# Laying out octets by batch with TensorE from a kept tile, in place of copies between partitions by DMA

## The chip, the cores and the metric

The kernel runs on one core of one Trainium2 chip. The metric is the device time of the execution in microseconds (us), taken as the median of the runs. The engines are named as in the profile: PE is TensorE (PEld its weight loads), DVE is VectorE, ACT is ScalarE, POOL is GpSimd and SP is SyncE, which here only issues DMAs.

## The reference

The input is q, k and v of shape (8 batches, 8 heads, 576 tokens, 64). An attention with exponential features gives x of shape (8, 576, 512), and a spectral mix then works on x:

```
X = rfft(x, axis=1)                                  # along the tokens
Y[:, :64] = Xr*w_r - Xi*w_i + 1j*(Xr*w_i + Xi*w_r)   # 64 modes, a 512 x 512 matrix each
y = irfft(Y, n=576, axis=1)
u = x + y
out = u + relu(u @ w_ch)
```

The weights w_r and w_i are 64 matrices of 512 x 512 each, 64 MB each in float32. All that follows concerns the second half, from the mix to the output.

## The kernel before, in words

**The two halves.** The first 300 us or so work through sixteen units of attention; each ends in a few matmuls that give the low frequencies of its tokens (tile XT). In between, and after the last unit, run the mixes.

**Mixes and octets.** A mix (function `mix`) multiplies one group g of 128 input channels by one load of weights of 1 MB (eight modes, real or imaginary). Two mixes (i = 0, 1) for each of four groups g make up the 512 output channels of an octet o: eight modes, with real and imaginary part and eight batches, so 128 rows in the order (mode and part, batch). There are eight octets. Of the 64 mixes twenty come after the last unit: the twelve for g = 3 of octets 0 to 5, then eight for octets 6 and 7. In the order of these twenty, counted from 0, octet o < 6 ends with mix 2 o + 1, octet 6 with mix 15 and octet 7 with mix 19. The loop `while mixq` goes through them; `left` is the number of mixes still to come.

**Weights.** `next_w` issues the load of the next weights from POOL's queue into a ring of nine tiles (`pw`, tag "wt") of 8 KB a partition. A load waits until a tile of the ring is free, which is when the mix that read it is done. The tiles `zall`, `yall` and `yl` come from the same ring; each takes its slot when it is first written.

**What an octet's end does.** The sum of the octet is put together in `yst` (two DVE adds of 256 columns). It is turned by four PE transposes into `yT` (one copy by ACT, one by DVE) and multiplied by w_ch (`wchb`, eight matmuls) to give z, which ACT and DVE cast into `zst`. The rows of `yst` and `zst` are in the order (mode and part, batch), but the inverse transform needs the modes on the partitions and one batch at a time. `put` does this by DMA: 128 rows of 1 KB go to sixteen partitions of `yall` (or `zall`), eight rows in each, one for each batch. For octets 6 and 7 further copies go into `yl`.

**Chunks and fills.** The tokens are 36 chunks, four pairs of batches bp by nine n. Before the sums can be put in, each chunk is turned and multiplied by w_ch (`hold`, a step of four transposes and four matmuls; its result goes to `xw`). After octet 5, every chunk takes up octets 0 to 5 (`Absorb`): one matmul from the inverse table CI or CD by `yall` of its batch, added to x by DVE (`keep_x`), and one by `zall`, added to `xw` by PE and ACT, or, for fourteen chunks that are left aside, by ACT and POOL (`keep_w`). The eight chunks of bp 0 with n < 8 are `early` and take octet 6 as well (112 rows instead of 96). Three chunks (`only_x`, `only_w`) keep the product with w_ch in PSUM until the sums come. All these steps stand in one list, `todo`, and `fill(n)` does n of them after a mix; n is worked out from what is left, so that the list is empty before the last mix. After the last mix, `Last` adds octets 6 and 7 and stores.

**Order.** Each engine does its instructions in the order of the program. PSUM has four single banks ("pt") and two double ones ("pp") in this part.

Of the kernel before, what the change touches and what calls it, by code (L numbers as in the profile page):

```python
# [11 lines left out]
BF16 = mybir.dt.bfloat16  # L12
# [5 lines left out]
B_, H_, S_, D_ = 8, 8, 576, 64  # L18
# [25 lines left out]
def kernel(  # L44
# [14 lines left out]
    pe, dve, act = (InOrder(tc, e) for e in (nc.tensor, nc.vector, nc.scalar))  # L59
    pool, sp = InOrder(tc, nc.gpsimd), InOrder(tc, nc.sync)  # L60
# [23 lines left out]
    pw = pw_cm.__enter__()  # L84
# [255 lines left out]
    def wload(g, w):  # L340
        wt = home(g, w)
        o, i = w // 2, w % 2
        w = (moe_w_r, moe_w_i)[i]
        pool.dma_start(
            wt.rearrange("p m r e -> p m (r e)"),
            w[MG * o:MG * o + MG, g * 128:(g + 1) * 128, :].rearrange(
                "m (p r) e -> p m (r e)", r=2))
        return wt
# [10 lines left out]
    def next_w(n):  # L359
        for _ in range(n):  # L360
            if wq:
                key = wq.pop(0)
                wts[key] = wload(*key)
# [25 lines left out]
    wchb = const.tile([128, 4, 512], BF16, name="wchb")  # L389
    CF = const.tile([128, 6, 2, 2, 32], BF16, name="CF")  # L390
    side = const.tile([128, 2, 4], F32, name="side")
    ident_b = const.tile([128, 128], BF16, name="ident_b")
# [32 lines left out]
    for t in range(3):  # L425
        r = slice(32 * t, 32 * t + 32)
        dve.tensor_scalar_mul(out=minus[r], in0=ident_f[r, r], scalar1=-1.0)
    every = mf[0:96, 0:32]
    for t in range(3):
        r = slice(32 * t, 32 * t + 32)  # L430
# [30 lines left out]
    def mix(g, w, wt, XT, bank):  # L461

        o, i = w // 2, w % 2
        late = g >= 2 and o >= 6
        first, last = i == 0 and not (late and g == 3), i == 1 and not (late and g == 2)
        if first:
            pys[o] = bank()
        py = pys[o]
        for r in range(2):
            for j in range(4):  # L470
                pe.matmul(
                    py[32 * j:32 * j + 32, :],
                    lhsT=XT[:, i, r, :, :, :, 4 * o + j].rearrange("p t x b -> p (t x b)"),
                    rhs=wt[:, j, r, :], start=(first and r == 0), stop=(last and r == 1),
                )
        if last and g == 0:
            act.copy(yacc[:, o, :], pys.pop(o))
        elif last and g < NG - 1:
            dve.tensor_tensor(
                out=yacc[:, o, :], in0=pys.pop(o), in1=yacc[:, o, :], op=ALU.add)  # L480
# [19 lines left out]
    def unit(i):  # L500
        return units[i] if 0 <= i < len(units) else None

    for n in range(-2, len(units) + 1):
        P, Q, K, R = (unit(n + i) for i in (-1, 0, 1, 2))
# [77 lines left out]
    def bank(shape=(128, DMODEL), dt=F32):  # L582
        return pst.tile(list(shape), dt, name="pt", tag="pt")
# [4 lines left out]
    pb_cm = tc.tile_pool(name="pb", bufs=2)  # L588
    pb = pb_cm.__enter__()
    xw = pb.tile([128, NP, 9, DMODEL], BF16, name="xw", bufs=1)  # L590
    zall = pw.tile([128, B_, DMODEL], BF16, name="zall", tag="wt")
    yall = pw.tile([128, B_, DMODEL], BF16, name="yall", tag="wt")
    yl = pw.tile([128, B_, DMODEL], BF16, name="yl", tag="wt")
# [85 lines left out]
    class Channels:  # L679
# [29 lines left out]
        def hold(self, pf):  # L709
            for g in range(NG):  # L710
                pe.matmul(pf, lhsT=self.xT[:, g, :], rhs=wchb[:, g, :],
                          start=(g == 0), stop=False)
# [68 lines left out]
    ch = [Channels(*c) for c in chunks]  # L781
    ab = [Absorb(*c) for c in chunks]
    K = len(ch) - 3
    full = sorted(ab[:K], key=lambda c: c.early)
    spare = []
    for c in full[0:28:2]:
        c.aside = True
# [17 lines left out]
        ch[i].hold(ab[i].q)  # L805

    todo = [ch[0].turn] + [lambda i=i: hold(i) for i in range(len(ch))]
    todo += [c.only_x for c in ab[K:]] + [c.only_w for c in ab[K:]] + [c.all for c in full]
    A = 3 * 3 + K

    def fill(n):
        for _ in range(n):
            if todo:
                todo.pop(0)()

    def put(src, o, dst, copies):
        if o < 7:
            sp.dma_start(dst[16 * o:16 * o + 16], src)
        if o > 5:
            for s in copies:  # L820
                r = 32 * s + 16 * (o - 6)
                (pool if o == 6 else sp).dma_start(yl[r:r + 16], src)


    class Last:
# [97 lines left out]
    while mixq:  # L923
        key = mixq.pop(0)
        g, o, i = key[0], key[1] // 2, key[1] % 2
        if key not in wts:
            next_w(1)
        if not mixq:
            assert not todo
            for c in seq[:2]:  # L930
                c.base(1)
            for c in (seq[0], seq[2]):
                c.base(0)
        mix(*key, wts.pop(key), XTb[g % 2], bank)
        next_w(1)
        left = len(mixq)
        if left > 8:
            n = -(-max(len(todo) - A - 2, 0) // (left - 8))
        elif left == 8:
            n = 2  # L940
        else:
            n = math.ceil(len(todo) / max(left - 0.6, 0.4)) if left else 0
        if g == NG - 1 and i == 1:
            end = left == 0
            py = pys.pop(o)
            yst = pb.tile([128, DMODEL], BF16, name="yst")
            pt = [bank([128, 2, 128], BF16) for h in range(2)]
            yT = [pb.tile([128, 2, 128], BF16, name=f"yT{h}") for h in range(2)]
            for h in range(2):
                dve.tensor_tensor(out=yst[:, H * h:H * h + H], in0=py[:, H * h:H * h + H],  # L950
                                  in1=yacc[:, o, H * h:H * h + H], op=ALU.add)
            put(yst, o, yall, (0, 2))
            if o < 5:
                fill(min(n, 1))
            for h in range(2):
                for dc in range(2):
                    pe.transpose(pt[h][:, dc, :],
                                 yst[:, H * h + 128 * dc:H * h + 128 * dc + 128], ident_b)
                if h:
                    dve.tensor_copy(yT[h], pt[h])  # L960
                else:
                    act.copy(yT[h], pt[h])
            if o < 5:
                fill(min(n - 1, 1))
            elif end:
                seq[0].straight(0)
                seq[0].keep_p()
                seq[2].straight(0, (0,))
            cut = (slice(0, 384), slice(384, DMODEL))
            pz = [bank([128, e.stop - e.start]) for e in cut]  # L970
            for e in range(2):
                for h in range(2):
                    for dc in range(2):
                        pe.matmul(
                            pz[e], lhsT=yT[h][:, dc, :], rhs=wchb[:, 2 * h + dc, cut[e]],
                            start=(h == dc == 0), stop=(h == dc == 1))
            zst = pb.tile([128, DMODEL], BF16, name="zst")
            act.copy(zst[:, cut[0]], pz[0])
            dve.tensor_copy(zst[:, cut[1]], pz[1])
            put(zst, o, zall, (1, 3))  # L980
            fill(max(n - 2, 0) if o < 5 else n)
        else:
            fill(n)
    assert not todo
# [18 lines left out]
    for g in range(3, len(seq)):  # L1003
        s, ts = seq[g], [seq[i] for i in ahead[g - 3:g - 2]]
# [49 lines left out]
```

## Time and profile before

| | |
|---|---|
| median of 3 runs | 439.06 us (438.94 to 439.31) |
| the profiled execution | 440.25 us, of which 438.5 us are the profile's span |
| mean granted clock of TensorE | 0.906 |
| PE, DVE, ACT, POOL busy | 332.0, 296.4, 279.4, 113.0 us |
| DMA | 99.55 MB moved, 227 GB/s on average |
| mix 0, mix 12, mix 19 start at | 302.1, 368.5, 403.1 us |
| copies yall<-yst and zall<-zst | 7 of 128 KB each, first issued at 320.40, last at 386.80 us |

The profile is one execution. Its span runs from the first instruction to the last; start times in the text are microseconds from the start of the span. A row's duration holds the time in which a matmul drains, during which the next one already runs, so that TensorE's rate is read from start to start.

### The profile page before, as it was taken

The page shows a single profiled execution, that of the slowest core. Times are in us where ns is not written, and L with a number is a line of the kernel's source. Part 1 is how long each engine was busy: PE and PEld are TensorE (multiplying, and loading weights), DVE is VectorE, ACT ScalarE, POOL GpSimd, SP SyncE. Part 2 cuts the span into 40 slices and gives each one's busy share as a digit, 9 for nine tenths or more (in the row PEclk, how much of TensorE's full clock was granted, in tenths as well). Part 3 has the DMA queues.
Part 4 walks back from the last instruction along what each step waited for, and adds up shares of the span by engine and source line. Part 5 has one row for each costly group of instructions (what it writes and reads, how often), then busy time and mean ns, then how long its engine had stood idle before and what let it go on. Part 6 is the DMA issues. An engine that isn't in the chain of part 4 may idle for free.

```text
span 438.5 us, 10107 instructions
## 1 busy us (share of the span) xinstructions
PE 332.0 (76%) x4190; PEld 202.1 (46%) x4233; DVE 296.4 (68%) x583; ACT 279.4 (64%) x478; POOL 113.0 (26%) x151
## 2 busy tenths in 40 slices
PE   2687678688687687687787787284789999998993
PEld 1355456465465465455465555152444554333320
DVE  5667776765786877976986888243784333886684
ACT  3786786776986886875875876210553442665781
POOL 6232132113221222221222221121101111483072
PEclk9998796789998999996996998876899999999996
DMA  9999999999999999999999999999999999996787
GB/s 213 209 212 210 237 212 237 237 212 248 228 211 239 225 228 232 237 215 235 232 217 239 210 239 211 238 213 212 212 215 223 219 222 224 212 219 135 242 361 309
DMA packets 51710, 99.55 MB, mean 227 GB/s; under 512 B 2512, under 2 KB 13648, under 8 KB 51664
## 3 DMA queue, kind: packets, MB, share of 16 engines
q0 software_dynamic: 45232, 85.86, 99.7%
q1 hardware_dynamic: 6272, 12.98, 8.5%
q8 instruction: 33, 0.54, 0.5%
q14 instruction: 13, 0.11, 0.1%
q10 hardware_dynamic: 160, 0.07, 0.1%
HBM read 163.64 MB, written 9.44 MB: 395 GB/s over the span
## 4 chain that ended last, share of the span: by engine, by line
PE 43%; DVE 22%; ACT 18%; DMA 10%; issue 5%; POOL 0%; POOLq 0%; ACTq 0%; DVEq 0%
PE pt L37 17%; PE one L37 14%; DMA wt<-in_moe_w_r_dram 8%; PE two L37 8%; ACT AB L37 7%; DVE m L37 6%; DVE mk L37 6%; PE pp L37 4%; ACT AQ L37 3%; ACT XT L37 3%; DVE xs L37 2%; DVE XT L37 2%; DMA qb<-in_q_dram 2%; ACT qT L37 1%; DVE yacc L37 1%
## 5 line engine op out<-in xcount | busy, mean ns | idle before, releaser
L37 ACT ACTIVATE AB<-two 128x1024 bf16<-128x1024 f32 x64 | 62.0, 1024 | 10.6 <-DVE mk L37 7.2
L37 ACT ACTIVATE AQ<-two 128x1024 bf16<-128x1024 f32 x64 | 62.6, 1043 | 2.0 <-PE two L37 1.8
L37 ACT CAST xw<-pt 128x512 bf16<-128x512 f32 x50 | 29.4, 588 | 41.9 <-PE pt L37 41.8
L37 DVE TENSOR_REDUCE m<-two 128x8 f32<-128x1024 f32 x32 | 39.2, 1224 | 15.8 <-PE two L37 15.7
L37 DVE TENSOR_TENSOR va<-vn,ee 128x1152 bf16<-128x1152 f32 x32 | 42.0, 1355 | 8.2 <-DMA vn<-in_v_dram 8.2
L37 DVE TENSOR_REDUCE mk<-two 128x8 f32<-128x1024 f32 x32 | 38.9, 1218 | 7.7 <-PE two L37 7.7
L37 POOL DMA_DIRECT2D wt<-in_moe_w_i_dram x28 | 21.0, 750 | 86.4 <-PE pt L37 37.7
L37 POOL DMA_DIRECT2D wt<-in_moe_w_r_dram x30 | 22.5, 751 | 69.2 <-PE one L37 30.7
L37 PE MATMUL pt<-wchb,xT 128*128 128x512 bf16 x127 | 35.6, 393 | 5.2 <-DVE xT L37 3.5
L37 PEld LDWEIGHTS <-xs 128*128 128x128 bf16 x624 | 31.6, 103 | 12.6 <-issue 7.3
L37 PE MATMUL two<-w2blk,qT 128*128 128x256 bf16 x128 | 22.1, 301 | 20.2 <-ACT AB L37 8.4
L37 ACT COPY qT<-one 128x512 bf16<-128x512 bf16 (+1 forms) x32 | 19.3, 641 | 27.5 <-PE one L37 27.2
L37 PEld LDWEIGHTS <-qT 128*128 128x128 bf16 x144 | 14.6, 103 | 36.8 <-issue 33.2
L37 PE MATMUL one<-wt,XT 128*32 128x512 bf16 x304 | 27.5, 452 | 4.9 <-DMA wt<-in_moe_w_i_dram 3.3
L37 PE MATMUL two<-mT,minus 96*128 96x512 bf16 x64 | 28.5, 446 | 3.2 <-issue 1.5
L37 PEld LDWEIGHTS <-AQ 128*128 128x128 bf16 x512 | 25.8, 111 | 8.8 <-issue 5.6
L37 PE MATMUL one<-kvz,AQ 128*128 128x65 bf16 x512 | 28.4, 212 | 1.2 <-ACT qT L37 0.8
L37 DVE COPY xT<-pt 128x512 bf16<-128x512 bf16 x36 | 17.0, 472 | 17.8 <-PE pt L37 17.8
L37 PE MATMUL one<-va,AB 64*128 64x65 bf16 x1024 | 22.5, 199 | 8.3 <-DVE va L37 8.3
L37 DVE RECIPROCAL rd<-one 128x6 f32<-128x6 f32 x48 | 9.4, 196 | 27.6 <-PE one L37 27.5
L37 DVE TENSOR_TENSOR xs<-one,rd 128x384 bf16<-128x384 f32 x48 | 26.7, 557 | 1.6
L37 POOL DMA_DIRECT2D kb<-in_k_dram x16 | 11.4, 714 | 62.2 <-PE one L37 57.2
(151 smaller groups left out, 719.3 us busy)
## 6 DMA issues: line engine op xcount, KB each, us to landing
wt<-in_moe_w_r_dram POOLq DMA_DIRECT2D x30, 1024.0 KB, 28.1
wt<-in_moe_w_i_dram POOLq DMA_DIRECT2D x28, 1024.0 KB, 28.4
out_dram<-of SPq DMA_DIRECT2D x16, 512.0 KB, 4.0
vn<-in_v_dram POOLq DMA_DIRECT2D x14, 576.0 KB, 24.6
kb<-in_k_dram POOLq DMA_DIRECT2D x16, 288.0 KB, 20.4
qb<-in_q_dram POOLq DMA_DIRECT2D x16, 288.0 KB, 18.3
xs<-in_moe_w_i_dram POOLq DMA_DIRECT2D x2, 1024.0 KB, 23.1
vn<-in_v_dram SPq DMA_DIRECT2D x2, 576.0 KB, 4.6
```

The source lines that it names most:

```text
L37: ins = f(*args, **kwargs)
```

## The change

A new tile `yTa` of the weight ring keeps the turned y of octets 0 to 5, and of octet 6 for batches 0 and 1, in the order (channels, batch, octet, mode and part). At the end of octets 0 to 5 the two copies out of PSUM write there instead of into `yT`, with the rows taken apart by batch; there is no product with w_ch, no `zst`, and no DMA. For octet 6, which still makes z for `yl`, two small DVE copies add its part.

A new step `relay(b)` makes `yall` and `zall` of batch b, with 96 rows (112 for batches 0 and 1): four transposes of the kept columns back into rows, which DVE copies to `yall`, and four matmuls of the same columns by w_ch, which ACT casts to `zall`. The eight relays are put into the list: those of batches 7 and 6 ahead of the three chunks held in PSUM, each other one right before the first chunk that needs it.

The list of chunks is sorted so that all nine of bp 0 come last (before, chunk (0, 8) came earlier). The steps of a fill at the end of octets 0 to 4, which stood partly between the sum and the transposes and partly before the product, now all come after the copies. Three calls of `next_w` are left out (after mixes 0, 10 and 11), so that slots come free for `yTa`, `yall` and `zall`; the two last loads are issued one mix later for it.

```diff
+    yTa = pw.tile([128, 4, B_, 7, 16], BF16, name="yTa", tag="wt")
     zall = pw.tile([128, B_, DMODEL], BF16, name="zall", tag="wt")
...
-    full = sorted(ab[:K], key=lambda c: c.early)
+    full = sorted(ab[:K], key=lambda c: c.bp == 0)
+
+    def relay(b):
+
+        at = slice(0, 6 + (b < 2))
+        n = 16 * at.stop
+        cols = [yTa[:, dc, b, at].rearrange("p o k -> p (o k)") for dc in range(4)]
+        pt, pz = bank([128, 4, 128], BF16), bank()
+        for dc in range(4):
+            pe.transpose(pt[:n, dc, :], cols[dc], ident_b)
+        for dc in range(4):
+            pe.matmul(pz[:n], lhsT=cols[dc], rhs=wchb[:, dc, :],
+                      start=(dc == 0), stop=(dc == 3))
+        dve.tensor_copy(yall[:n, b], pt[:n].rearrange("p c e -> p (c e)"))
+        act.copy(zall[:n, b], pz[:n])
...
-    todo += [c.only_x for c in ab[K:]] + [c.only_w for c in ab[K:]] + [c.all for c in full]
-    A = 3 * 3 + K
+    order2 = [c.only_x for c in ab[K:]] + [c.only_w for c in ab[K:]]
+    laid = {7, 6}
+    tail = [lambda: relay(7), lambda: relay(6)] + order2
+    for c in full:
+        bs = {2 * c.bp, 2 * c.bp + 1} if c.n == 8 else {2 * c.bp + c.n // 4}
+        tail += [lambda b=b: relay(b) for b in sorted(bs - laid)] + [c.all]
+        laid |= bs
+    A = 3 + len(tail)
+    todo += tail
...
-    def put(src, o, dst, copies):
-        if o < 7:
-            sp.dma_start(dst[16 * o:16 * o + 16], src)
-        if o > 5:
-            for s in copies:
-                r = 32 * s + 16 * (o - 6)
-                (pool if o == 6 else sp).dma_start(yl[r:r + 16], src)
+    def put(src, o, copies):
+        for s in copies:
+            r = 32 * s + 16 * (o - 6)
+            (pool if o == 6 else sp).dma_start(yl[r:r + 16], src)
...
-        next_w(1)
         left = len(mixq)
+        if left not in (19, 9, 8):
+            next_w(1)
...
-            put(yst, o, yall, (0, 2))
-            if o < 5:
-                fill(min(n, 1))
+            if o > 5:
+                put(yst, o, (0, 2))
             for h in range(2):
                 for dc in range(2):
                     pe.transpose(pt[h][:, dc, :],
                                  yst[:, H * h + 128 * dc:H * h + 128 * dc + 128], ident_b)
+                src = pt[h].rearrange("p c (k b) -> p c b k", b=B_)
+                into = yTa[:, 2 * h:2 * h + 2, :, o] if o < 6 else None
                 if h:
-                    dve.tensor_copy(yT[h], pt[h])
+                    dve.tensor_copy(*((into, src) if o < 6 else (yT[h], pt[h])))
                 else:
-                    act.copy(yT[h], pt[h])
-            if o < 5:
-                fill(min(n - 1, 1))
-            elif end:
+                    act.copy(*((into, src) if o < 6 else (yT[h], pt[h])))
+            if o < 6:
+                fill(n)
+                continue
+            if o == 6:
+                for h in range(2):
+                    dve.tensor_copy(
+                        yTa[:, 2 * h:2 * h + 2, 0:2, 6],
+                        yT[h].rearrange("p c (k b) -> p c b k", b=B_)[:, :, 0:2])
+            if end:
...
-            put(zst, o, zall, (1, 3))
-            fill(max(n - 2, 0) if o < 5 else n)
+            put(zst, o, (1, 3))
+            fill(n)
```

More of the change, by code (lines that the diff above doesn't have):

```diff
@@ L947 @@
             pt = [bank([128, 2, 128], BF16) for h in range(2)]
-            yT = [pb.tile([128, 2, 128], BF16, name=f"yT{h}") for h in range(2)]
+            yT = [pb.tile([128, 2, 128], BF16, name=f"yT{h}") if o > 5 else None
+                  for h in range(2)]
             for h in range(2):
```

## The prediction

> **What bounds the kernel now.** I read the page's queue table first, then the chain that ended last in order of time, then busy time by stretches, then the single rows of TensorE, VectorE and ScalarE around the places that the change touches.
>
> The queue table makes the weight stream look like the bound:
>
> ```profile
> q0 software_dynamic: 45232, 85.86, 99.7%
> q1 hardware_dynamic: 6272, 12.98, 8.5%
> ```
>
> The queue that carries the weights (q0) is busy for the whole span. But what ends last is read from the chain, and there the DMA stops at 302 us; from then on TensorE carries it, in pieces like the second of these (start, length, both in us), with short ones of VectorE and ScalarE between:
>
> ```profile
> 265.36 36.71 DMA wt<-in_moe_w_r_dram
> ...
> 357.56 5.21 PE pt L37 x41
> ```
>
> I number the last twenty mixes 0 (starts 302.1) to 19 (starts 403.1). Stage A is mixes 0 to 12, in which octets 0 to 5 end (after mixes 1, 3, 5, 7, 9, 11); stage B is from mix 12 to mix 19, where the octets' sums are put into the chunks. By stretches (us, then PE, PEld, DVE, ACT, POOL busy, clock, DMA share, GB/s):
>
> ```profile
> 351.07:360.47 9.40, 9.12 (x77) 4.83 (x77) 3.63 (x10) 4.27 (x8) 1.48 (x2) 1.00 1.12 220
> ...
> 373.95:403.11 29.16, 27.40 (x160) 10.29 (x160) 22.83 (x38) 20.65 (x38) 18.29 (x18) 1.00 1.03 203
> ```
>
> TensorE is busy 9.12 of 9.40 us in stage A with VectorE and ScalarE under half, and 27.4 of 29.2 in stage B, with VectorE (22.8) and ScalarE (20.7) close behind. So every TensorE microsecond added or removed here counts. The weights are only just ahead: the last load is issued at 369.47 and lands 32.8 us later, at 402.3, under a microsecond before mix 19; but no mix after number 0 waits for one.
>
> **What is removed, stage A.** Each of octets 0 to 5 loses eight z matmuls, two zst casts and two copies by DMA. TensorE's rows in order of time at an octet's end, with a hold step put between mix and y transposes (octet 4, from 355.02) and with nothing between (octet 5, from 363.35):
>
> ```profile
> 355.02 0.67 PE L37 MATMUL pt<-wt,XT 128*32 128x512 bf16 x8
> 355.62 0.40 PE L37 MATMUL pt<-ident_b,xs 128*128 128x128 bf16 x4
> 355.86 0.81 PE L37 MATMUL pt<-wchb,xT 128*128 128x512 bf16 x3
> 356.72 0.39 PE L37 MATMUL pt<-ident_b,yst 128*128 128x128 bf16 x4
> 356.94 0.39 PE L37 MATMUL pt<-ident_b,xs 128*128 128x128 bf16 x4
> 357.56 1.02 PE L37 MATMUL pt<-wchb,xT 128*128 128x512 bf16 x4 [0.23 <-ACT xw L37]
> ...
> 363.35 0.66 PE L37 MATMUL pt<-wt,XT 128*32 128x512 bf16 x8
> 364.54 0.61 PE L37 MATMUL pt<-ident_b,yst 128*128 128x128 bf16 x4 [0.54 <-DVE yst L37]
> 365.35 1.05 PE L37 MATMUL pt<-wchb,yT 128*128 128x384 bf16 x8 [0.19 <-ACT yT L37]
> 366.23 0.39 PE L37 MATMUL pt<-ident_b,xs 128*128 128x128 bf16 x4
> 366.45 1.03 PE L37 MATMUL pt<-wchb,xT 128*128 128x512 bf16 x4
> 367.32 0.39 PE L37 MATMUL pt<-ident_b,xs 128*128 128x128 bf16 x4
> ```
>
> Counted from start to next start (a row's time holds the drain, which overlaps): eight z matmuls 0.88 (365.35 to 366.23), four transposes 0.22, four 512-column matmuls 0.87 (366.45 to 367.32), so 0.217 each; a hold step is 0.22 + 0.87 = 1.09; a mix with the gap ahead of it 0.69. Two mixes, six hold steps, four y transposes, the z matmuls and 0.39 of wait for a bank (from 356.94 + 0.22 to 357.56, ended by ACT) make 1.38 + 6.54 + 0.22 + 0.88 + 0.39 = 9.41; the stretch from mix 8 to mix 10 is 9.40. So the accounting closes.
>
> The diff also takes away the hold step between mix and y transposes: the fills of octets 0 to 4 now come after both copies. TensorE then waits for VectorE's sums, as octet 5 does already: the mix's eight matmuls are issued by 363.95 (0.60 after their start, as 355.02 to 355.62), the transposes end at 365.15, and the next matmul could start 0.17 before that, at 364.98 (as 356.94 lies 0.17 before the end of the row at 356.72): 1.04 for the octet's end instead of 0.22. The wait lets ScalarE empty its bank, so the 0.39 goes. New cycle 1.38 + 6.54 + 1.04 = 8.96, a gain of 0.44 for each of octets 2, 3 and 4: 1.3. Octet 5 had nothing between: it gains 0.88 + 0.19 = 1.07. Octets 0 and 1 lie in 302 to 332 where VectorE works on the inverse tables (22.6 of 30.2 busy) and is often what ends TensorE's wait; I take 0.3 each. Stage A: **-3.0 us** (from -1.1, octet 5 alone, to -5.5, all six by 0.88 and that wait).
>
> The copies from turned y to the kept tile, with a strided PSUM side, stay at 0.29 on DVE and 0.38 on ACT or grow a little (the strided xT copies take 0.64 where the plain ones take 0.42); both engines idle half of this stage. Nothing. The fourteen copies of 128 KB (1.8 MB, some 8 us of the stream's 220 GB/s) leave the 16 DMA engines: weights land earlier, which is worth nothing as no mix waits for them. SP has nothing else queued there before the yl copies and the stores. The three skipped loads give the slots for the kept tile and for yall and zall; the loads (3,10) to (2,15) move one mix earlier or stay, the last is released after mix 13 instead of 12, but by then the stream still has five loads before it: nothing. On POOL they stand ahead of the sums of the chunks that leave xw aside, as before.
>
> **What is added, stage B.** Eight relays, each four transposes (0.22), four 512-column matmuls (0.87), a DVE copy of turned y (0.41, as a plain xT copy) and an ACT cast of z (0.59, as an xw cast). TensorE alone: 8 x 1.09 = 8.7. More comes from where they stand: six stand right ahead of the chunk that reads their result. The state of the two other engines when such a relay begins, r, is read where TensorE is through with an odd chunk, at r = 383.27:
>
> ```profile
> 383.31 0.68 DVE L37 TENSOR_TENSOR xs<-pt,xs 128x512 bf16<-128x512 f32 x1
> ```
> ```profile
> 383.91 0.59 ACT L37 CAST xw<-pt 128x512 bf16<-128x512 f32 x1
> ```
>
> DVE is free at r + 0.72 and has yall at r + 1.13, just behind the last z matmul (r + 1.09): hidden. ACT is free at r + 1.23; the z product is ready at r + 1.25; cast 0.59, so zall is there at r + 1.9 and the chunk's z matmul, which without a relay would start at r + 0.22 (behind one y matmul, since these chunks leave xw aside), starts at r + 1.94. So an exposed relay costs 1.72. Four are fully exposed (batches 4, 5, 2, 3): 6.9; batch 1 stands before a chunk with one more matmul in between: 1.5; batch 0 is the last item of its fill and mix 17 covers the cast: 1.1; batches 7 and 6 stand together and cover each other, with a little wait for banks while the held sums occupy one of four: 2.4. Sum 11.9. Something comes back: chunks go by VectorE's 0.60 each (380.30, 380.90, 381.50 in its rows), TensorE needs 0.54 (five matmuls of 0.217 for two); 33 x 0.06 = 2.0 of such waiting is in stage B, and each relay lets VectorE catch up. I take back 1.2. The two small DVE copies for octet 6 lie beside its z matmuls: nothing, and 0.3 without that cover. Stage B: **+10.7 us** (from 8.7 - 2.0 = 6.7, all latency hidden, to 15.4, every relay at 1.72 and its transposes at the 0.10 of a weight load instead of 0.055).
>
> Against the row (four transposes in 0.22) stands a rule of the Trainium skill, TensorE: Matmul & The Clock Gate, Part 4: PE-mode transpose: about 275 ns for one 128 x 128 transpose inside a kernel, and a copy out of PSUM behind it. By that an estimate of 32 x 0.22 = 7 us would come on top, to about +15; in this trace transposes follow each other at 0.055, so I go by the row.
>
> **Sum:** -3.0 + 10.7 = +7.7, with ends +1.2 and +14.3. On the profiled execution: 438.5 + 7.7 = 446.2 of span and, with the 1.75 around it, 448.0; it is 1.2 above the median of the runs (440.25 against 439.06), so the median goes to **446.8 us**. The stores after mix 19 move with it unchanged.
>
> **The rivals.**
> - Relays mostly hidden. Stage B has VectorE near its limit; if relays fill only the gaps there, the low end holds, +1.2 to +4: about 441. For it: VectorE's steps of 0.60. Against: the cast of z can't begin before the z product ends. 0.14.
> - Faster: the weight stream paces mixes 13 to 19. Landings are 0.8 to 4 us ahead of them (mix 13: 371.3 and 374.0; mix 19: 402.3 and 403.1). If the pace were really the stream's, 8.3 us less of copies would pull mix 19 forward by 8 and the added TensorE work (8.7 - 5.3 = 3.4) would be paid from that: 439.1 - 8 + 3.4 = 434.5. It decides where the wait for a weight is longer than the wait for TensorE; the waits show only one DMA wait of TensorE after 302, 4.3 us at mix 0. 0.07.
> - The kept tile gets its slot late, so that the change doesn't do what it says. It comes from the ring of nine weight slots, and the first yall copy shows what that can mean: its data were there at 310.9, but it was issued at 320.40, right after mix 2 gave a slot. If ACT and DVE wait so for the kept tile, TensorE runs on for about 2 of these 9.5 us until its four banks are full: 7.5 more, 454. The skipped first load should prevent it. 0.08.
>
> ```profile
> 320.40 0.70 SPq L37 DMA_DIRECT2D yall<-yst  x1
> ```
>
> **How the numbers follow.** The forecast as worked out, +4 to +12 (443 to 451): 0.68. Rivals 0.14, 0.07, 0.08; 0.03 for no difference in time. Under 0.2% (0.9 us) a measurement of this kernel can't tell from no change. Faster: 0.07. Same: 0.03 and the bottom of the first rival, 0.05. Slower: 0.88. The range 441.5 to 452 leaves out the faster rival, the late slot and the lowest part of the hidden case, together under 0.2.
>
> **What would show it.** In the profile after: no yall<-yst or zall<-zst transfers; from mix 4 to mix 10 a cycle of about 9.0 instead of 9.4 per octet; mix 12 near 365.5; in stage B eight groups of a 96- or 112-row transpose and product, and behind six of them TensorE waiting about 0.6 us for ACT zall; mix 19 near 411; weights landed by some 395. I am wrong if TensorE waits for DMA wt after mix 0, if ACT's first copy into the kept tile waits for a mix, or if the waits behind the relays are missing.

## The result, and the profile after

The changed kernel takes 452.03 us (median of 4 runs, 451.44 to 452.41) where the kernel before takes 439.17 in the same comparison: the ratio is 1.0292, 95% interval 1.0274 to 1.031. That is 12.9 us slower. The profiled execution took 451.44 us with a span of 449.6, which is 11.1 us over the span before.

The queue table of the page after, for the weights (q0) and for the copies and stores (q1):

```profile
q0 software_dynamic: 45232, 85.86, 97.2%
q1 hardware_dynamic: 4256, 11.14, 6.8%
```

The copies are gone (q1 moved 12.98 MB before, 11.14 now), and q0 is through earlier: its share of the span is 97.2% where it was 99.7%. The cycle of one octet (two mixes) of stage A and the time from the first relay to mix 19, by stretches (us, then PE, PEld, DVE, ACT, POOL busy, clock, DMA share, GB/s):

```profile
344.02:352.98 8.96, 8.18 (x67) 4.17 (x68) 3.64 (x9) 3.88 (x7) 1.48 (x2) 1.00 1.12 211
...
368.41:415.00 46.59, 39.25 (x226) 16.68 (x227) 27.54 (x50) 25.22 (x46) 19.03 (x19) 1.00 0.63 124
```

The cycle is 8.96 us instead of 9.40. Stage B has no engine busy for nearly all of its time: the DMA share is 0.63, VectorE is busy for 27.5 of 46.6 us, and TensorE, which was busy for 94% of its stretch before, for 84%. So it is not one engine that is full; they wait for each other.

From the starts of the mixes in TensorE's rows in order of time, for all kernels (us; the experiments follow below):

| kernel | mix 0 to 4 | 4 to 12 | 12 to 19 | after 19 | span |
|---|---|---|---|---|---|
| before | 30.16 | 36.23 | 34.61 | 35.39 | 438.5 |
| after | 29.74 | 33.67 | 50.23 | 34.60 | 449.6 |
| e1_nocopy | 28.70 | 39.51 | 35.99 | 35.40 | 441.3 |
| e5_nocopy_pool | 28.69 | 36.22 | 34.63 | 35.12 | 436.4 |
| e2_hoist | 28.72 | 33.68 | 45.65 | 34.67 | 444.2 |
| e3_swap | 28.73 | 33.66 | 49.09 | 34.67 | 447.8 |
| e6_pp | 30.06 | 33.68 | 47.86 | 34.69 | 447.8 |
| e4_between | 28.32 | 32.36 | 50.24 | 34.69 | 446.9 |
| e8_all | 27.10 | 32.32 | 43.90 | 34.71 | 439.7 |
| e9_all_front | 28.38 | 31.19 | 43.32 | 34.59 | 439.2 |
| e10_y_by_dma | 27.11 | 34.94 | 41.70 | 35.76 | 440.9 |
| e7_onebank | 30.14 | 35.00 | 35.42 | 36.79 | 438.7 |
| e11_onebank_nocopy | 30.12 | 35.01 | 34.61 | 35.25 | 436.7 |
| e12_order | 30.15 | 36.22 | 34.98 | 35.31 | 438.9 |

The first column isn't firm: after, e2, e3 and e6 have the same instructions up to mix 12 and show 28.72 to 30.06 there. The same four show 33.66 to 33.68 in the second, so the reading rests on the two middle columns, which repeat to 0.02 us where the instructions are the same. The last differs by 0.28 between e1 and e5, which differ only ahead of it.

The loss is one number: mixes 12 to 19 take 15.6 us more. Two relays of that stretch in TensorE's rows, batch 5 from 377.81 and batch 3 from 390.73:

```profile
377.81 0.39 PE L37 MATMUL pt<-ident_b,yTa 128*96 128x128 bf16 x4
378.70 1.02 PE L37 MATMUL pt<-wchb,yTa 128*96 128x512 bf16 x4 [0.50 <-DVE xs L37]
379.56 0.38 PE L37 MATMUL pp<-yall,CD 96*128 96x512 bf16 x1
380.40 0.38 PE L37 MATMUL pp<-zall,CD 96*128 96x512 bf16 x1 [0.45 <-ACT zall L37]
...
390.73 0.39 PE L37 MATMUL pt<-ident_b,yTa 128*96 128x128 bf16 x4
390.95 1.03 PE L37 MATMUL pt<-wchb,yTa 128*96 128x512 bf16 x4
391.81 0.38 PE L37 MATMUL pp<-yall,CI 96*128 96x512 bf16 x1
392.65 0.38 PE L37 MATMUL pp<-zall,CI 96*128 96x512 bf16 x1 [0.45 <-ACT zall L37]
```

Behind both, the chunk's z matmul waits for ACT's cast: 0.62 us beyond start-to-start (391.81 + 0.22 to 392.65). Ahead of the product of batch 5, but not of batch 3, there is a second wait of 0.67 (377.81 + 0.22 to 378.70), for VectorE's sum of the chunk before. VectorE's rows at the same place:

```profile
377.97 0.68 DVE L37 TENSOR_TENSOR xs<-pt,xs 128x512 bf16<-128x512 f32 x1
378.57 0.41 DVE L37 COPY yall<-pt 96x512 bf16<-96x512 bf16 x1
380.81 0.69 DVE L37 TENSOR_TENSOR xs<-pp,xs 128x512 bf16<-128x512 f32 x1 [1.83 <-PE pp L37]
```

The sum of 377.97 ends at 378.65, and then the product starts: TensorE waited for the bank that this sum reads. After the copy of y, VectorE stands idle for 1.83 us, although the chunk's x product was issued at 379.56. It starts at 380.81, when the z matmul of 380.40 is through (0.38 later): x and z of such a chunk share a double bank, and its x sum comes only behind both.

Counted from start to start over the whole stretch: eight relays of 1.09 make 8.7; five waits for the cast of z (0.61, 0.62, 0.61, 0.62, 0.40) 2.9; five waits for a bank inside relays (batches 6, 5, 2, 0, 1: 0.61, 0.67, 0.67, 0.65, 0.41) 3.0; at the three held chunks 0.61 and 0.84 where the kernel before has 0.73 (372.13 + 0.43 to 373.30) and 0.16 (373.95 + 0.59 to 374.70), so 0.6 more; the new order of the chunks 0.4 (e12 below: 34.98 against 34.61). Together 15.5 of the 15.6.

### The profile page after: what moved, and what is told of

Read it like the earlier page. It is cut to its first block, busy times and chain, and to the rows that moved or that the text cites. A ratio compares the mean times of both kernels' runs of the same rounds, so it can differ in the third digit from the quotient of the medians.

```text
span 449.6 us, 10088 instructions
## 1 busy us (share of the span) xinstructions
PE 335.6 (75%) x4205; PEld 203.7 (45%) x4249; DVE 299.5 (67%) x587; ACT 281.3 (63%) x480; POOL 112.6 (25%) x151
## 3 DMA queue, kind: packets, MB, share of 16 engines
q0 software_dynamic: 45232, 85.86, 97.2%
q1 hardware_dynamic: 4256, 11.14, 6.8%
## 4 chain that ended last, share of the span: by engine, by line
PE 40%; DVE 20%; ACT 17%; DMA 15%; issue 6%; POOL 1%; POOLq 0%; ACTq 0%; DVEq 0%
PE pt L37 17%; PE one L37 13%; DMA wt<-in_moe_w_r_dram 8%; ACT AB L37 7%; DMA vn<-in_v_dram 7%; PE two L37 6%; DVE mk L37 4%; DVE m L37 4%; PE pp L37 4%; ACT AQ L37 4%; DVE xs L37 3%; ACT XT L37 2%; ACT qT L37 1%; DVE xw L37 1%; DVE XT L37 1%
## 5 line engine op out<-in xcount | busy, mean ns | idle before, releaser
L37 PE MATMUL one<-wt,XT 128*32 128x512 bf16 x304 | 28.6, 468 | 5.1 <-DMA wt<-in_moe_w_i_dram 3.5
L37 PE MATMUL two<-mT,minus 96*128 96x512 bf16 x64 | 27.6, 430 | 3.2 <-issue 1.3
L37 PEld LDWEIGHTS <-XT 128*32 128x32 bf16 x512 | 14.4, 149 | 28.6 <-issue 22.4
L37 PE MATMUL two<-w2blk,kT 128*128 128x256 bf16 x128 | 20.9, 291 | 8.6 <-ACT AB L37 8.6
```

What stands on the lines that cost most here:

```text
L37: ins = f(*args, **kwargs)
```

## The experiments

**Are the copies worth anything? (e1, e5)** Both are the kernel before without its fourteen copies.

```diff
     def put(src, o, dst, copies):
-        if o < 7:
-            sp.dma_start(dst[16 * o:16 * o + 16], src)
...
+        if left in (8, 7):
+            dve.memset((zall, yall)[left - 7], 0.0)
```

> The kernel before, with its fourteen copies into yall and zall left out and the two tiles set to zero by one VectorE memset each (so the octets 0 to 6 are missing from the output). Theory, TensorE sets the pace after mix 0 and the copies cost nothing: 439.2 us as before, within 1 us. Rival, the copies hold back the weight stream and through it the mixes: up to 8 us less, 431 to 435.

443.73 us, ratio 1.0102 (1.0079 to 1.0125). Neither number: the stretches show why. From mix 13 to mix 19 it takes 29.16 us, as before; the loss lies between mixes 11 and 13, where VectorE's two memsets stand ahead of the sum of octet 5 and of the last turned chunks (VectorE's rows):

```profile
362.64 1.76 DVE L37 MEMSET yall<- 128x2048 uint32 x1 [1.51 <-PE pt L37]
364.32 0.69 DVE L37 TENSOR_TENSOR yst<-pt,yacc 128x256 bf16<-128x256 f32 x2
```

So this run measured its memsets. e5 has them on GpSimd (`pool.memset`, in float32):

> As the run without the fourteen copies, but GpSimd, which is idle between the last load and the first sums, sets yall and zall to zero (octets 0 to 6 are missing from the output). Theory, the copies cost nothing and what that run lost was VectorE's time in the two memsets: 439.4 us, within 1. Rival, taking the copies away costs or gains time by itself: 443 again, or 431 to 435.

438.4 us, ratio 0.9991 (0.9974 to 1.0007). Mixes 4 to 12 and 12 to 19 take 36.22 and 34.63 us, with the copies 36.23 and 34.61. In the kernel before, fourteen copies cost TensorE nothing after mix 4, and taking them away brings nothing that the runs can tell from no change.

**Are the waits behind the relays latency? (e2)**

```diff
         laid |= bs
+    for i in [i for i, f in enumerate(tail) if i > 1 and f.__name__ == "<lambda>"]:
+        tail.insert(i - 2, tail.pop(i))
```

> The changed kernel with six of its eight relays (batches 4, 5, 2, 3, 0, 1) two steps earlier in the list; nothing else moves. Theory, what the relays cost above their TensorE work is latency: the waits for the cast of z (five, 2.9 us in all) go, and of the bank waits (3.0 us) some, since an even chunk's x sum no longer comes late behind z: 446.7 to 449.1 us, taken 448. Rival, the relays' own TensorE work and VectorE's pace are all of it: 452.0, within 0.7.

447.1 us, ratio 1.0184 (1.0167 to 1.0201); stage B is 4.58 us shorter. The relay of batch 5 and what follows it, in TensorE's rows:

```profile
374.40 0.42 PE L37 MATMUL pt<-ident_b,yTa 128*96 128x128 bf16 x4
374.66 1.03 PE L37 MATMUL pt<-wchb,yTa 128*96 128x512 bf16 x4
375.52 0.38 PE L37 MATMUL pp<-yall,CD 96*128 96x512 bf16 x1
375.74 0.38 PE L37 MATMUL pp<-zall,CD 96*128 96x512 bf16 x1
```

None waits. The same work in another order is 4.9 us faster by the medians (4.6 in stage B); the rival, that work and VectorE's pace are all of it, is out.

**Is it the bank, or VectorE's pace? (e3, e6)** e3 turns the order inside a relay round:

```diff
-        pt, pz = bank([128, 4, 128], BF16), bank()
-        for dc in range(4):
-            pe.transpose(pt[:n, dc, :], cols[dc], ident_b)
+        pz, pt = bank(), bank([128, 4, 128], BF16)
         for dc in range(4):
             pe.matmul(pz[:n], lhsT=cols[dc], rhs=wchb[:, dc, :],
                       start=(dc == 0), stop=(dc == 3))
+        for dc in range(4):
+            pe.transpose(pt[:n, dc, :], cols[dc], ident_b)
```

> The changed kernel with the order inside a relay turned round: the four products first, then the four transposes; the product's bank is taken first. Theory, a relay finds only one free bank of four, since octet 6 or 7 holds one from its first mix to its end: the product now gets the free bank, its cast runs beside the wait for the second bank, and the waits inside the relays (0.4 to 0.7 us each, 3.0 in all) go, while the chunk behind now waits about as long for yall as before for zall: 449 to 450.5 us. Rival, banks are not short and the wait is VectorE's pace, which no order changes: 452.0, within 0.7.

451.62 us, ratio 1.0277 (1.0243 to 1.0311), so by the medians not told from 452.0; stage B is 1.14 us shorter. The relay of batch 5:

```profile
377.82 1.03 PE L37 MATMUL pt<-wchb,yTa 128*96 128x512 bf16 x4
378.70 0.38 PE L37 MATMUL pt<-ident_b,yTa 128*96 128x128 bf16 x4
379.60 0.38 PE L37 MATMUL pp<-yall,CD 96*128 96x512 bf16 x1 [0.51 <-DVE yall L37]
379.81 0.38 PE L37 MATMUL pp<-zall,CD 96*128 96x512 bf16 x1
```

The wait inside the relay is gone, as the theory has it, but the wait behind it, now for yall, is 0.68 (378.70 + 0.22 to 379.60) instead of 0.62, and mixes 12 to 13, with the relays of batches 7 and 6, take 0.67 more. The order alone doesn't settle it. e6 keeps the order and gives the product another bank:

```diff
-        pt, pz = bank([128, 4, 128], BF16), bank()
+        pt = bank([128, 4, 128], BF16)
+        pz = bank() if b > 5 else banks()[:, 0]
```

> The changed kernel, but the product of the relays of batches 4, 5, 2, 3, 0 and 1 goes into one of the double banks instead of a second single one. Theory, a relay waits for its second bank because one of the four single banks is held by octet 6 or 7: the waits inside four relays (0.67, 0.67, 0.65, 0.41) go: 449.6 us, 449 to 450.5. Rival, it is VectorE's pace and the wait only moves on to the next sum: 452.0, within 0.7.

449.4 us, ratio 1.0227 (1.0213 to 1.0241), and stage B is 2.37 us shorter; the four waits named in the expectation add up to 2.40. It is the bank. One of the four single banks holds the products of octet 6 from mix 12 to mix 15 and of octet 7 from mix 16 on. The relay of batch 3 stands right after octet 6's end, when no octet holds a bank, and doesn't wait in the changed kernel either. Nor does that of batch 4: there a bank is held, but VectorE has been idle for 1.73 us, so no x sum still holds another. It takes both, the held bank and a late sum.

**The octet's end (e4)** puts the hold step back between the sum and the transposes:

```diff
             if o > 5:
                 put(yst, o, (0, 2))
+            if o < 5:
+                fill(min(n, 1))
...
             if o < 6:
-                fill(n)
+                fill(n - 1 if o < 5 else n)
```

> The changed kernel with one hold step put back between the sum and the y transposes of octets 0 to 4, as the kernel before has it; the other steps stay behind the copies. Theory, TensorE sets the pace of this stage: 0.82 us less for each of octets 2, 3 and 4 if no bank wait comes, 0.43 if the 0.39 of before comes back, and less than that for octets 0 and 1: 1.3 to 4.1 us less, 448 to 450.7. Rival, the weights pace the stage and the wait is only filled: 452.0, within 0.7.

448.77 us, ratio 1.0219 (1.0194 to 1.0245). Mixes 4 to 12 take 32.36 us, 1.31 less, which is 0.44 for each of three octets: the cycle is 8.53. In it the wait of the kernel before is back (TensorE's rows):

```profile
343.79 0.39 PE L37 MATMUL pt<-ident_b,yst 128*128 128x128 bf16 x4
344.01 0.39 PE L37 MATMUL pt<-ident_b,xs 128*128 128x128 bf16 x4
344.63 1.02 PE L37 MATMUL pt<-wchb,xT 128*128 128x512 bf16 x4 [0.23 <-ACT xw L37]
```

That is the lower of the two numbers of the expectation; at this pace the weights do not hold up the stage.

**All waits hidden (e8, e9).** e8 takes e2, e4 and e6 together, with one bank and one VectorE copy for the turned y of octets 0 to 4:

> The changed kernel with all that should hide its waits: relays two steps earlier, their product in a double bank, the hold step between sum and transposes, and one bank for the turned y of octets 0 to 4. Theory, what stays is TensorE's added work, 8.7 us of relays against 5.3 us of removed products, less the waits that the kernel before has: 441 to 443 us, still over the kernel before. Rival, with the waits hidden the freed DMA pays: under 439.

441.52 us, ratio 1.0049 (1.0035 to 1.0063), as expected. But one of the waits left is new: mix 12 waits for its weights, although no copies run (TensorE's rows):

```profile
361.09 0.67 PE L37 MATMUL pt<-wt,XT 128*32 128x512 bf16 x8 [1.03 <-DMA wt<-in_moe_w_r_dram]
```

So here TensorE, 59.4 us from mix 0 to mix 12, has caught up with the weight stream; in the kernel before this takes 66.4. e9 also puts the relays of batches 7 and 6 ahead of the held chunks, with their product in a double bank:

```diff
     A = 3 + len(tail)
-    todo += tail
+    todo[-3:-3] = tail[:2]
+    todo += tail[2:]
```

> As the run with all waits hidden, and the relays of batches 7 and 6 stand ahead of the three chunks that hold banks, with their product in a double bank too. Theory, waits for banks are still 0.6 and 0.6 us behind these two relays and 0.8 at the held sums: 1.2 to 1.8 less, 439.7 to 440.6 us. Rival, these waits move on to the held chunks: 441.5.

441.03 us, ratio 1.0028 (1.0013 to 1.0042). The gain is 0.5 instead of 1.2 to 1.8 by the medians, and 0.58 lies between mixes 12 and 19. TensorE doesn't wait for weights in e9, but it comes to mix 4 later (28.38 against 27.10): from mix 0 to mix 12 the two take nearly the same, 59.57 and 59.42. Stage B is now 43.32 us: 8.71 more than before, and the relays' own work is 8 x 1.09 = 8.72. That the two agree to 0.01 is in part chance, as the new order of the chunks alone makes 0.37 (e12). But with the waits hidden little beyond TensorE's work is left in stage B, and that is more than stage A saves.

**y by DMA, z by TensorE (e10).** e9 with the seven copies of y and without the relays' transposes; the loads make room for yall one mix earlier.

```diff
-        pt = bank([128, 4, 128], BF16)
         pz = banks()[:, 0]
-        for dc in range(4):
-            pe.transpose(pt[:n, dc, :], cols[dc], ident_b)
...
+        if o < 7 and copies[0] == 0:
+            sp.dma_start(yall[16 * o:16 * o + 16], src)
...
-        if left not in (19, 9, 8):
+        if left not in (19, 18, 8):
```

> As the run before it in this list, but y goes into yall by the seven DMA copies of the kernel before, and the relays make z alone, without the transposes. Theory, TensorE's work sets the pace and seven copies fit beside the weights: 8 x 0.22 = 1.8 us less than that run, 438 to 439 us, at or just under the kernel before. Rival, the stream is at its limit with any copies, so that the last mixes wait for weights: no less than that run, 440 or more.

442.62 us, ratio 1.0063 (1.0044 to 1.0082). Stage B is 1.62 us shorter, close to the 1.8, but mixes 11 and 12 wait for weights (TensorE's rows):

```profile
358.51 0.66 PE L37 MATMUL pt<-wt,XT 128*32 128x512 bf16 x8 [2.51 <-DMA wt<-in_moe_w_i_dram]
...
363.44 0.66 PE L37 MATMUL pt<-wt,XT 128*32 128x512 bf16 x8 [0.96 <-DMA wt<-in_moe_w_r_dram]
```

The time is the rival's. In e8, without copies, mix 12 starts 59.42 us after mix 0, in e10 62.05, which is 2.6 later; the five copies of octets 0 to 4 are 3 us of the stream at 215 GB/s (an estimate). In both kernels the DMA share is 1.12 from 302 to 390 us, which is full, so the stream never ran dry, which speaks against the later loads as the cause; a run with the later loads alone was not made.

**The kernel before with a bank less (e7, e11).**

```diff
-            pt = [bank([128, 2, 128], BF16) for h in range(2)]
+            if o < 5:
+                pall = bank([128, 4, 128], BF16)
+                pt = [pall[:, 0:2], pall[:, 2:4]]
...
+                        dve.tensor_copy(yTw, pall)
```

> The kernel before, but the turned y of octets 0 to 4 takes one single bank instead of two and one VectorE copy empties it. Theory, the 0.39 us that TensorE waits for ACT in each of these octets is for that bank: 0.39 less for octets 2, 3 and 4 and perhaps for 0 and 1: 437.3 to 438.2 us. Rival, the wait moves to the later copy of the turned y: 439.4.

439.36 us, ratio 1.0007 (0.9997 to 1.0017): the rival's time, but not for its reason. Mixes 4 to 12 take 35.00 us, 1.23 less; the wait for the bank is gone. Of this gain 0.81 is lost in stage B, at mix 19 (TensorE's rows; the rest goes after mix 19, in this profile at least, whose execution took 440.5 us):

```profile
401.91 0.66 PE L37 MATMUL pt<-wt,XT 128*32 128x512 bf16 x8 [0.72 <-DMA wt<-in_moe_w_i_dram]
```

> The kernel before with one bank for the turned y and without the fourteen copies (GpSimd sets yall and zall to zero; octets 0 to 6 are missing from the output). Theory, in the run with one bank alone TensorE gained 1.2 us by mix 12 and lost it at mix 19 to the last weights, whose stream the copies hold back; without them the gain stays: 437.0 to 438.0 us. Rival, the wait at mix 19 has nothing to do with the copies: 439.4.

438.06 us, ratio 0.9961 (0.9945 to 0.9976). With one bank less and no copies the gain of mixes 4 to 12 stays (35.01) and mix 19 waits for no weight (34.61 for stage B). Leaving the copies out also lets yall and zall take their slots of the ring later, so that the last load is issued at 359.84 us instead of 367.46. But the DMA share is 1.12 from 302 to 390 us in both kernels: the stream never runs dry, which speaks for what it has to move, and not the time of issue, as what delays the last weights (landed at 396.4 without copies, 401.9 with them). From mix 0 to mix 19 it is 101.00 us before, 100.56 in e7 and 99.74 in e11. So the copies begin to cost as soon as TensorE gets some half microsecond faster.

**The new order of chunks alone (e12).**

```diff
-    full = sorted(ab[:K], key=lambda c: c.early)
+    full = sorted(ab[:K], key=lambda c: c.bp == 0)
```

> The kernel before with only the new order of the chunks: chunk (0, 8) comes last with the others of its pair. Theory, this part alone makes what the changed kernel shows behind its relays, 0.35 us more between mixes 18 and 19 and 0.8 less after mix 19: 439.0 us, 438.6 to 439.4. Rival, the shorter end comes from the missing copies, so that the order alone costs 0.35: 439.8.

440.71 us beside 440.68 for the kernel before on that chip, ratio 1.0005 (0.999 to 1.002). The 0.36 between mixes 18 and 19 is there; the shorter end is not (35.31).

## Why the prediction was right or wrong

The direction and its reason held: TensorE sets the pace after mix 0, and the change gives it more work. The size was too small: 446.8 us forecast, 452.03 measured, at the upper end of the range, 452.

**Stage A, -3.0:** mixes 0 to 12 took 66.39 us before and 63.41 after, -2.98. That this agrees to 0.02 is partly luck, as mixes 0 to 4 (-0.4, where -0.6 was taken) move by more than a microsecond for the same instructions. The firm part is mixes 4 to 12: -2.56, where 1.3 + 1.07 = 2.4 was worked out. The cycle came out at the 8.96 that was worked out, with TensorE waiting for the sum. e4 confirms the step from the other side: with the hold step put back the 0.82 goes and the 0.39 returns.

**The copies, nothing:** right as a term (e5), and too simple as a statement. There was 0.8 us between the last landing and mix 19; e7 and e11 show that TensorE could gain about half a microsecond before the copies would have begun to count, and e8 that without copies, too, the stream is soon the limit.

**The relay's work, 8 x 1.09:** right; e9 shows it bare, 8.71.

**An exposed relay, 1.72:** right where its assumptions held. Batch 3: z matmul at r + 1.92 against r + 1.94.

**The steps that failed** are two terms of stage B. The first is the banks. The working had no wait between a relay's transposes and its product, and "a little wait" of 0.2 for batches 7 and 6. It counted four single banks in stage B, and named only the held sums as taking one; but the product of octet 6 or 7 is in another from its first mix to its end. That term is 3.0 inside the relays and 0.6 more at the held chunks, against 0.2. e6 took 2.37 of it away by a bank alone. The second is the 1.2 that was to come back because each relay lets VectorE catch up. The accounting has no place for it: an x sum waits for the z matmul of its double bank, so that VectorE stood idle while the cast was made (1.83 us in the row shown), and its lag then held the bank that the next relay wanted. That this lag is the reason is read from the rows, not tried by itself. These corrections, 3.4 and 1.2, with the 0.4 of the new order, which the working left out, add up to 5.0; stage B (+10.7 forecast, +15.6 measured) was missed by 4.9. The high end given for stage B, 15.4, comes to 15.2 by its own terms (8 x 1.72 + 32 x 0.045).

**The rivals.** Relays mostly hidden: no; nothing hides the work, and only e8 and e9, with another order and other banks, come near the 441 that it named. The weight stream as pace: no; no mix after number 0 waits for a weight in the changed kernel. The late slot: no; ACT's first copy into the kept tile waited for no mix.

**The rule weighed against the row.** The Trainium skill (TensorE: Matmul & The Clock Gate, Part 4: PE-mode transpose) would have put 7 us on top for the transposes. The relays show four in 0.22 (390.73 to 390.95), 0.055 each, so the row was the better guide. That the rule's sum of about +15 lies nearer to the total is chance: the missing time stood in waits.

**Left open:** in all kernels whose relays make both y and z, the end after mix 19 is some 0.7 us shorter (34.6 to 34.7 against 35.4). The order of chunks alone doesn't do that (e12: 35.31), nor does leaving out the copies (e1: 35.40, e5: 35.12); what does was not found.

## What to carry to other kernels

When a copy by DMA is replaced with work on a compute engine, first ask whether anybody waits for that copy; here nobody did, and 8.7 us of TensorE work were bought with 5.3. Count the PSUM banks that are free at each place, with the accumulators that live across several steps, before taking a latency as hidden, and look whether two results that share a bank make an engine wait for the later one. And where two limits lie within a microsecond of each other, as the weight stream and TensorE do here, relieving either alone brings next to nothing: only e11, which relieved both (and left out the laying-out), was clearly faster than the kernel before.

## What the runs showed of the hardware

- Weight loads of fewer columns were not shorter. All instructions on the kept tile, by operation (durations in ns: least, median, most):

```profile
L37 PEld LDWEIGHTS <-yTa x64: 119/123/131, 368.2 to 407.8; 128*96 128x96 bf16 x48, 128*112 128x112 bf16 x16
L37 PE MATMUL pt<-ident_b,yTa x32: 216/219/257, 368.4 to 406.9; 128*96 128x128 bf16 x24, 128*112 128x128 bf16 x8
...
L37 DVE COPY yTa<-pt x6: 424/424/426, 310.5 to 362.7; 128x256 bf16<-128x256 bf16 x6
```

  The loads of 96 and 112 columns take 119 to 131 ns (median 123) where those of yst with 128 columns take 98; four transposes still follow each other in 0.22 us, so it cost nothing here.
- The VectorE copy that reads PSUM with a stride of eight, and writes runs of sixteen elements, takes 0.42 us where the plain one took 0.29 for the same 256 columns. The ACT copy of the same form takes 0.37, where the plain one took 0.38.
- In e7 the granted clock is 0.89 from 402 to 418 us, after the wait at mix 19; before and in e11 it is 1.00 there. The end after mix 19 is 1.4 us longer in e7, and the eight z matmuls there take 1.71 us (404.45 to 406.16) where octet 5's took 0.88 before. That the wait lowers the clock fits this one profile and was not tried by itself.
